# A planned attention-and-MLP kernel on one core: the first step's weights loaded ahead of the chunks, wider zero products, and part of VectorE's early work on ScalarE

## The chip, the core and the metric

The kernel runs on one core of a Trainium2 chip. The core has five engines that run side by side, each through its own list of instructions in order: TensorE (PE in the profile; PEld is its loading of the stationary operand), VectorE (DVE), ScalarE (ACT), GpSimd (POOL) and SyncE (SP), which here only issues transfers. They wait for each other by semaphores. Sixteen DMA engines move data from and to HBM. The metric is the device time of one execution in microseconds; the median of three runs of the kernel before is 622.57 us.

## What is computed

The input is `q`, `k`, `v` of shape (4, 8, 768, 64), a decay `lam` per head, and two weight matrices. A decayed linear attention runs in blocks of 64 positions, and its result goes through a two-layer MLP with a squared ReLU:

```python
for b in range(nb):                      # 12 blocks of 64 positions
    intra = einsum(qb, kb) * Dmask       # Dmask = lam ** rel below the diagonal
    intra = einsum(intra, vb)
    inter = einsum(qb * lam_pow, kv_state)
    out[:, :, sl] = intra + inter
    kv_state = lam_block * kv_state + einsum(kb * rev_pow, vb)
...
h = maximum(x @ w_in, 0)                 # x: 3072 x 512, w_in: 512 x 2048
return (h * h) @ w_out                   # w_out: 2048 x 512
```

## The kernel before

**Work.** The 3072 tokens are 24 chunks of 128 (two attention blocks of one batch each); three chunks make a tile, so there are 8 tiles. The hidden width 2048 is 16 steps of 128. One FFN step of one tile is a first product `mm1` (12 matmuls on 384 columns, lines 429), a ReLU and a square, and a second product `mm2` (lines 435, 436, 438). All matrices of the FFN are kept as a rounded part and a rest (`wih`/`wil`, `woh`/`wol`, `gh`/`gl`), hence three products for each.

**A chunk.** Two transfers of 512 KB bring `ka` and `qv`. `weighted` multiplies the values by the decay table `wdec` that GpSimd makes with two `pow` instructions from the small input `lamx`: for the first six chunks half of the eight head slices on ScalarE (line 326), the rest in one VectorE instruction (line 328). `open` (line 299, matmuls `bank<-qv,ka`) forms scores and state increments; `opened` adds up the states (`hold`, lines 351, 352, 358) and masks the scores (`s`, line 359); `result` (line 299, `bank<-s,qv` and `bank<-qv,hold`) runs in two parts around a tiny ScalarE copy `dot` (line 397); VectorE scales the outcome by `rdec` into `xr` (line 405), ScalarE rounds it into `xs` (line 411) and VectorE takes the rest (line 412).

**Weights.** The matrices arrive as 64-bit floats, 512 KB for each half of a step (32 loads into three buffers `st`). `weights(f, i)` turns a half into float32: ScalarE `Abs` (line 276), four VectorE instructions (lines 277 to 283), a ScalarE cast (line 285) and a VectorE subtraction (line 287). Half 0 of step f is `wih`/`wil`, half 1 is `woh`/`wol`.

**Order.** Nothing is scheduled by a compiler. `Plan` records every operation with an engine, a duration, a key, dependences and buffers, and `Plan.order` plays a list schedule with those numbers; the kernel then issues the instructions in the order that came out. Changed numbers in the plan therefore change the order on the engines, not only the numbers' own lines. Where the plan sees TensorE idle before 140 us of its own time, it writes products of zeros (`filler`, line 237 on 128 rows, line 240 on two halves of 64) into the order. The loads of the first six chunks and the first weights get keys from `load_at` and `ws_at`; a smaller key goes first on SyncE's queue.

Each float32 matmul of lines 237 to 252 and 299 appears twice in the profile's count, together with two loads of the stationary operand: 15 zero products in the order are 30 MATMUL rows and 30 LDWEIGHTS rows.

Of the kernel before, what the change touches and what calls it, by code (L numbers as in the profile page):

```python
# [17 lines left out]
B, H, S, D = 4, 8, 768, 64  # L18
DM, DFF = 512, 2048
P = 128  # L20
# [35 lines left out]
class Plan:  # L56


    LAT = {"PE": 0.22, "ACT": 0.14, "DVE": 0.13, "POOL": 0.12, "SP": 2.3}

    def __init__(self):
        self.ops, self.slots = [], {}
# [11 lines left out]
    def order(self, pe_slow, fill, begin):  # L74
        need, out = {}, {}
        for o in self.ops:
            both = set(map(id, o.deps)) | set(map(id, o.after))
            need[id(o)] = len(both)
            for d in both:
                out.setdefault(d, []).append(o)  # L80
        ready = {e: [o for o in self.ops if o.eng == e and not need[id(o)]] for e in self.LAT}
        free = dict(dict.fromkeys(self.LAT, 0.0), **begin)
        slots = {k: [(0.0, i) for i in range(n)] for k, n in self.slots.items()}
        done, filled, mode = [], 0, None
        while any(ready.values()):
            best = None
            for e, ops in ready.items():
                can = []
                for o in ops:
                    t = max([free[e]] + [d.end + d.lat for d in o.deps])  # L90
                    want = {}
                    for b in o.bufs:
                        if b.slot is None:
                            want[b.kind] = want.get(b.kind, 0) + 1
                    ok = True
                    for k, n in want.items():
                        if len(slots[k]) < n:
                            ok = False
                            break
                        t = max(t, sorted(slots[k])[n - 1][0] + 0.15)  # L100
                    if ok:
                        can.append((t, o))
                if not can:
                    continue
                soon = max(free[e], min(t for t, _ in can)) + 0.05
                t, o = min(((t, o) for t, o in can if t <= soon), key=lambda x: (x[1].key, x[0]))
                if best is None or t < best[0]:
                    best = (t, o)
            assert best is not None, "no operation can get its buffers"
            t, o = best  # L110
            if o.eng == "PE" and t < fill:
                while free["PE"] + (long := FILL * (2.0 if free["PE"] < pe_slow else 1.0)) + FILL_REST < t:
                    bank = min(slots["bank"], default=(t, 0))
                    if bank[0] > free["PE"]:
                        break
                    done.append(Op("PE", long, 0, lambda i=bank[1], m=mode: self.filler(i, m != "A"), [], [], [], 0, None))
                    done[-1].start, done[-1].end = free["PE"], free["PE"] + long
                    free["PE"] += long
                    filled += 1
            dur = o.dur * (2.0 if o.eng == "PE" and t < pe_slow else 1.0)  # L120
            if o.mode:
                dur += SWITCH * (mode not in (None, o.mode))
                mode = o.mode
            o.start, o.end = t, t + dur
            free[o.eng] = o.end
            for b in o.bufs:
                if b.slot is None:
                    slots[b.kind].sort()
                    b.slot = slots[b.kind].pop(0)[1]
                b.left -= 1  # L130
                b.end = max(b.end, o.end + o.lat)
                if not b.left:
                    slots[b.kind].append((b.end, b.slot))
            ready[o.eng].remove(o)
            done.append(o)
            for d in out.get(id(o), ()):
                need[id(d)] -= 1
                if not need[id(d)]:
                    ready[d.eng].append(d)
        assert len(done) - filled == len(self.ops), "operations need each other"  # L140
        return done
# [6 lines left out]
F_LATE = 9  # L148

FIRST, SLOW_STEP, LAG, BEGIN2, CHUNK, STEP = 18.0, 6.5, 16, 9.0, 3.0, 4.8  # L150
PE_SLOW, FILL_END, FILL, FILL_REST, SWITCH = 10.0, 140.0, 0.215, 0.1, 0.18
XOFF = 16
AFTER = NF - 2


# [14 lines left out]
def kernel(ctx: ExitStack, tc: tile.TileContext, ka, qv, lamx, w, out):  # L170
# [61 lines left out]
    def power(hs):  # L232
        nc.gpsimd.tensor_tensor(out=wdec[:, hs], in0=lam[:, hs], in1=ej[:, hs], op=ALU.pow)  # L233

    def filler(i, full):
        if full:
            nc.tensor.matmul(tiles["bank"][i][:, 0:P], zero[:, 0:P], zero[:, P:2 * P], start=True, stop=True)
            return
        for h in range(2):
            nc.tensor.matmul(tiles["bank"][i][half(h), 0:P], zero[half(0), 0:HC], zero[half(0), P:2 * P], start=True, stop=True)  # L240

    plan.filler = filler

    o_start = plan.op("POOL", 5.2, -99, start_tables)
    o_pow = plan.op("POOL", 1.62, -98, lambda: power(slice(0, H)), [o_start])
    o_pow2 = plan.op("POOL", 1.62, -97, lambda: power(slice(H, 2 * H)), [o_pow])
    o_lc = plan.op("POOL", 1.01, -96, lambda: nc.gpsimd.tensor_tensor(out=lc, in0=lam[:, 2 * H:2 * H + NP], in1=ec, op=ALU.pow), [o_pow2])
    wb, rps = Buf("m"), Buf("bank")

# [10 lines left out]
    def weights(f, i, key, load_key):  # L260
# [11 lines left out]
        def add(eng, dur, fn, deps, bufs, lat=None):  # L272
            return plan.op(eng, dur, key, fn, deps, bufs, lat=lat)

        o = plan.op("SP", 1.6, load_key, lambda: nc.sync.dma_start(out=at(st), in_=w[f, i]), [], [st])
        o = add("ACT", 0.56, lambda: nc.scalar.activation(at(m), words(1).bitcast(F32), AF.Abs), [o], [st, m])  # L276
        o = add("DVE", 0.336, lambda: nc.vector.tensor_scalar(
            out=at(m), in0=at(m), scalar1=W_MIN, scalar2=W_MAX, op0=ALU.max, op1=ALU.min), [o], [m])
# [22 lines left out]
    class Chunk:  # L301
# [8 lines left out]
            self.blocks = 2 if self.c < NC_ - 1 else 1  # L310

        def load(self, key):
            self.o_ka = in_turn("load", plan.op("SP", 1.6, key, lambda: nc.sync.dma_start(out=at(self.ka), in_=ka[self.i]), [], [self.ka]))
            self.o_qv = in_turn("load", plan.op("SP", 1.6, key, lambda: nc.sync.dma_start(out=at(self.qv), in_=qv[self.i]), [], [self.qv]))

        def vals(self):
            return at(self.qv)[:, 1].rearrange("p n (h d) -> p n h d", h=2)
# [3 lines left out]

        def weighted(self, key):
            v = lambda: at(self.qv)[:, 1].rearrange("p n (h d) -> p (n h) d", h=2)
            split = H // 2 if self.i < N_ALONE else 0

            self.o_vd = [plan.op("ACT", act(D) + 0.11, key, lambda i=i: nc.scalar.mul(v()[:, i], v()[:, i], wdec[:, i:i + 1]), [self.o_qv, o_pow], [self.qv])
                         for i in range(split)]
            self.o_vd.append(plan.op("DVE", tt((H - split) * D), key, lambda: nc.vector.tensor_tensor(  # L328
                out=v()[:, split:], in0=v()[:, split:], in1=wdec[:, split:H].unsqueeze(2).broadcast_to([P, H - split, D]), op=ALU.mult), [self.o_qv, o_pow], [self.qv]))
# [12 lines left out]
        def opened(self, o, key):  # L342

            s0, s1 = state.get(self.b), Buf("hold")
            self.states, self.o_states = [s0 and s0[0], s1], [s0[1]] if s0 else []
            u = lambda t: at(self.sc[t])[:, NP * HC:].rearrange("p (n d) -> p n d", n=NP)

            def add(t, old, new, deps):

                if old is None:  # L350
                    return plan.op("DVE", tt(256), key, lambda: nc.vector.tensor_copy(at(new), u(t)), [o], [self.sc[t], new])
                return plan.op("DVE", tt(256), key, lambda: nc.vector.tensor_tensor(out=at(new), in0=u(t), in1=at(old), op=ALU.add), [o] + deps, [self.sc[t], new, old])  # L352

            self.o_states.append(add(0, self.states[0], s1, self.o_states))
            if self.blocks == 2:
                new = Buf("hold")
                o1 = add(1, s1, new, self.o_states[-1:])
                state[self.b] = (new, plan.op("DVE", tt(256), key, lambda: nc.vector.tensor_tensor(out=at(new), in0=at(new), in1=lc.unsqueeze(2).broadcast_to([P, NP, D]), op=ALU.mult), [o1, o_lc], [new]))
            self.o_s1 = [in_turn("mask", plan.op("DVE", tt(256), key, lambda h=h: nc.vector.tensor_tensor(
                out=at(self.s1[h]), in0=at(self.sc[h])[:, 0:NP * HC].rearrange("p (n i) -> p n i", n=NP), in1=mask.unsqueeze(1).broadcast_to([P, NP, HC]), op=ALU.mult),  # L360
                [o], [self.sc[h], self.s1[h]])) for h in range(2)]

        def result(self, g, ys):

# [104 lines left out]
                plan.op("SP", 1.0, key, lambda b=b, c=c, row=row: nc.sync.dma_start(  # L469
                    out=out[b * S + c * C:b * S + (c + 1) * C, :], in_=row()), [o], [ob])  # L470

    load_at = [0, 1, 2, 4, 6, 7]
    ws_at = [3, 5] + [8 + f for f in range(NF)]
    per = [SLOW_STEP, SLOW_STEP] + [STEP] * (len(TILES) - 2)
    begin = [FIRST, FIRST + LAG * SLOW_STEP]
    for ti in range(2, len(TILES)):
# [1 line left out]
    ws = []  # L478
    for f in range(NF):
        t = FIRST + f * SLOW_STEP  # L480
        ws.append((weights(f, 0, t - 7, -30 + ws_at[f]), weights(f, 1, t - 2, -30 + ws_at[f] + (2.5 if f == 1 else 0.5))))

    xs_, ready = [Buf("x") for _ in TILES], [[] for _ in TILES]
    chunks = []
# [72 lines left out]
```

## Time and profile before

| | before |
|---|---|
| median of 3 runs (lowest, highest) | 622.57 us (621.34, 624.99) |
| time of the profiled execution | 620.3 us |
| span, first to last instruction, of that execution | 618.5 us |
| mean granted TensorE clock | 0.994 |
| TensorE busy | 607.8 us, 98% of the span |
| VectorE busy | 300.1 us, 49% |
| ScalarE busy | 210.6 us, 34% |
| read from HBM, written | 41.96 MB, 6.29 MB |

In the profile's chain that ended last, time is followed back from the last instruction: at each step to whatever released it. "Issue" in it is time in which an engine waited for nothing that the profile shows. The table of windows gives busy microseconds and, in brackets, the number of instructions of each engine in each stretch, then the granted TensorE clock, the share of DMA time and the rate.

### The profile page before, as it was taken

What the parts mean: (1) busy time and instruction counts of PE and PEld (TensorE: products, weight loads), DVE (VectorE), ACT (ScalarE), POOL (GpSimd) and SP (SyncE); (2) the same over time, 40 slices, a digit from 0 to 9 for tenths busy, and PEclk for the clock granted to TensorE, in tenths of its full rate; (3) what the DMA queues carried; (4) which work ended last, traced back from release to release, by engine and by line L of the source; (5) the groups of instructions that cost most, each with busy time, mean ns of one, the idle gap of its engine ahead of it and who ended that gap; (6) DMA issues with size and microseconds to landing.
All of it is one profiled execution on the core that took longest, in us unless ns stands there. A gap on an engine that the chain in (4) does not pass through costs nothing.

```text
span 618.5 us, 13218 instructions
## 1 busy us (share of the span) xinstructions
PE 607.8 (98%) x5846; PEld 548.1 (89%) x5846; DVE 300.1 (49%) x616; ACT 210.6 (34%) x434; POOL 5.1 (1%) x10
## 2 busy tenths in 40 slices
PE   6899999999999999999999999999999999999997
PEld 6889898988898898998899998989898999899996
DVE  4699999975323444343343442434443433232223
ACT  3347786753342322222223232222223222232221
POOL 3000000000000000000000000000000000000000
PEclk9799999999999999999999999999999999999999
DMA  8465555516110122020121120112210000010001
GB/s 340 174 241 171 171 170 176 195 50 214 62 42 22 65 70 69 35 86 13 57 70 51 70 69 1 69 52 70 69 61 28 34 0 2 1 51 2 1 0 52
DMA packets 15177, 49.10 MB, mean 79 GB/s; under 512 B 1808, under 2 KB 1808, under 8 KB 15120
## 3 DMA queue, kind: packets, MB, share of 16 engines
q1 hardware_dynamic: 14976, 48.24, 22.3%
q8 instruction: 46, 0.75, 0.5%
q14 instruction: 11, 0.09, 0.1%
q10 hardware_dynamic: 144, 0.01, 0.0%
HBM read 41.96 MB, written 6.29 MB: 78 GB/s over the span
## 4 chain that ended last, share of the span: by engine, by line
PE 95%; DMA 2%; issue 1%; DVE 0%; ACT 0%; POOL 0%; POOLq 0%; SPq 0%; ACTq 0%
PE bank L429 43%; PE bank L435 14%; PE bank L438 14%; PE bank L436 14%; PE bank L299 8%; PE bank L240 2%; DMA qv<-qv 1%; DMA st<-w 1%; DMA g<-lamx 1%; POOL wdec L233 0%; POOLq L553 0%; PE bank L252 0%; DVE xr L468 0%; DVE qv L328 0%; ACT m L276 0%
## 5 line engine op out<-in xcount | busy, mean ns | idle before, releaser
L429 PE MATMUL bank<-xs,wih 128*128 128x384 f32 x1024 | 200.5, 338 | 0.0
L429 PEld LDWEIGHTS bank<-xs,wih 128*128 128x128 f32 x1024 | 180.6, 188 | 6.5 <-issue 0.2
L443 ACT ACTIVATE g<-bank 128x384 f32<-128x384 f32 x128 | 62.8, 491 | 271.9 <-PE bank L429 271.7
L449 DVE TENSOR_TENSOR g<-g 128x384 f32<-128x384 f32 x96 | 53.5, 558 | 207.2 <-ACT gh L448 161.5
L435 PE MATMUL bank<-woh,gh 128*128 128x512 f32 x384 | 152.0, 396 | 0.0
L436 PE MATMUL bank<-wol,gh 128*128 128x512 f32 x384 | 150.8, 393 | 0.0
L429 PE MATMUL bank<-xs,wil 128*128 128x384 f32 x512 | 110.1, 337 | 0.0
L438 PE MATMUL bank<-woh,gl 128*128 128x512 f32 x384 | 109.3, 393 | 0.1
L429 PEld LDWEIGHTS bank<-xs,wil 128*128 128x128 f32 x512 | 91.1, 188 | 0.0
L438 PEld LDWEIGHTS bank<-woh,gl 128*128 128x128 f32 x384 | 71.7, 188 | 16.9 <-DVE gl L450 1.0
L435 PEld LDWEIGHTS bank<-woh,gh 128*128 128x128 f32 x384 | 72.1, 188 | 14.1
L436 PEld LDWEIGHTS bank<-wol,gh 128*128 128x128 f32 x384 | 72.1, 188 | 13.4
L450 DVE TENSOR_TENSOR gl<-g,gh 128x384 fp32r<-128x384 f32 x128 | 71.3, 557 | 22.2 <-ACT gh L446 13.7
L448 ACT ACTIVATE gh<-g 128x384 fp32r<-128x384 f32 x96 | 50.3, 524 | 3.0
L411 ACT CAST xs<-xr 128x512 fp32r<-128x512 f32 x24 | 14.9, 621 | 46.6 <-DVE xr L405 46.6
L352 DVE TENSOR_TENSOR hold<-bank,hold 128x256 f32<-128x256 f32 x40 | 16.7, 418 | 25.9 <-PE bank L299 25.8
L328 DVE TENSOR_TENSOR qv<-qv,wdec 128x512 f32<-128x512 f32 (+1 forms) x24 | 15.0, 624 | 28.1 <-DMA qv<-qv 23.9
L299 PE MATMUL bank<-qv,ka 64*64 64x64 f32 x1472 | 28.3, 224 | 0.0
L299 PEld LDWEIGHTS bank<-qv,ka 64*64 64x64 f32 x1472 | 26.1, 140 | 0.6 <-issue 0.4
L276 ACT ACTIVATE m<-st 128x512 f32<-128x512 f32 x32 | 21.6, 675 | 8.0 <-DMA st<-w 7.8
L299 PEld LDWEIGHTS bank<-s,qv 64*64 64x64 f32 x768 | 17.8, 138 | 7.3 <-issue 5.3
L299 PE MATMUL bank<-s,qv 64*64 64x64 f32 x768 | 23.5, 232 | 0.3 <-ACT dot L397 0.3
(46 smaller groups left out, 310.7 us busy)
## 6 DMA issues: line engine op xcount, KB each, us to landing
st<-w SPq DMA_DIRECT2D x32, 512.0 KB, 3.5
ka<-ka SPq DMA_DIRECT2D x24, 512.0 KB, 3.7
qv<-qv SPq DMA_DIRECT2D x24, 512.0 KB, 5.2
out<-ob SPq DMA_DIRECT2D x23, 256.0 KB, 2.3
out<-xr SPq DMA_DIRECT2D x1, 256.0 KB, 2.0
g<-lamx ACTq DMA_DIRECT2D x1, 12.0 KB, 4.1
```

What stands on the lines that cost most here:

```text
L276: o = add("ACT", 0.56, lambda: nc.scalar.activation(at(m), words(1).bitcast(F32), AF.Abs), [o], [st, m])
L299: nc.tensor.matmul(*args, **kw, skip_group_check=True)
L328: self.o_vd.append(plan.op("DVE", tt((H - split) * D), key, lambda: nc.vector.tensor_tensor(out=v()[:, split:], in0=v()[:, split:], in1=wd ...
L352: return plan.op("DVE", tt(256), key, lambda: nc.vector.tensor_tensor(out=at(new), in0=u(t), in1=at(old), op=ALU.add), [o] + deps, [self.s ...
L429: nc.tensor.matmul(at(h)[:, 0:N], wt[:, cc, :], xt[:, cc, :], start=k == 0, stop=k == 3 * NCC - 1)
L435: nc.tensor.matmul(at(os_[j]), at(gh)[:, sl], woh[f], start=f == 0, stop=False)
L436: nc.tensor.matmul(at(os_[j]), at(gh)[:, sl], wol[f], start=False, stop=False)
L438: nc.tensor.matmul(at(os_[j]), at(gl)[:, sl], woh[f], start=False, stop=f == NF - 1)
L443: orr = plan.op("ACT", 0.49, key, lambda: nc.scalar.activation(at(g), at(h)[:, 0:N], AF.Relu), [o1], [h, g, run])
L448: ogh = plan.op("ACT", 0.525, key, lambda: nc.scalar.activation(at(gh), at(g), AF.Square), [orr], [g, gh])
L449: og = plan.op("DVE", 0.555, key, lambda: nc.vector.tensor_tensor(out=at(g), in0=at(g), in1=at(g), op=ALU.mult), [orr, ogh], [g])
L450: ogl = plan.op("DVE", 0.555, key, lambda: nc.vector.tensor_tensor(out=at(gl), in0=at(g), in1=at(gh), op=ALU.subtract), [og, ogh], [g, gh, ...
```

## The change

Four things are edited, and the plan's numbers with them:

1. `load_at` and `ws_at` put both halves of step 0's weights ahead of every chunk, and half 0 of step 1 between chunks 1 and 2; the conversions follow in the order, since the plan lets them start when they land.
2. A zero product may have 128, 256, 384 or 512 columns; the plan writes one wide product where it wrote up to four narrow ones.
3. `split` goes from 4 to 6 (`VS`): for the first six chunks six of eight head slices are weighted on ScalarE. The first state of a batch is copied from PSUM by ScalarE instead of VectorE (four copies). Score masks are taken for half 1 first.
4. The plan's own numbers: load 1.6 to 1.28, latency after a load 2.3 to 2.0, the GpSimd table 5.2 to 4.95, `PE_SLOW` 10 to 6.5. They set no instruction, only the order.

```diff
-    LAT = {"PE": 0.22, "ACT": 0.14, "DVE": 0.13, "POOL": 0.12, "SP": 2.3}
+    LAT = {"PE": 0.22, "ACT": 0.14, "DVE": 0.13, "POOL": 0.12, "SP": 2.0}
...
-                while free["PE"] + (long := FILL * (2.0 if free["PE"] < pe_slow else 1.0)) + FILL_REST < t:
+                while True:
+                    unit = FILL * (2.0 if free["PE"] < pe_slow else 1.0)
+                    n = min(4, int((t - FILL_REST - free["PE"]) / unit))
                     bank = min(slots["bank"], default=(t, 0))
-                    if bank[0] > free["PE"]:
+                    if n < 1 or bank[0] > free["PE"]:
                         break
...
-PE_SLOW, FILL_END, FILL, FILL_REST, SWITCH = 10.0, 140.0, 0.215, 0.1, 0.18
+PE_SLOW, FILL_END, FILL, FILL_REST, SWITCH = 6.5, 140.0, 0.215, 0.1, 0.18
+VS = 6
...
-            nc.tensor.matmul(tiles["bank"][i][half(h), 0:P], zero[half(0), 0:HC], zero[half(0), P:2 * P], start=True, stop=True)
+            nc.tensor.matmul(tiles["bank"][i][half(h), 0:n * P], zero[half(0), 0:HC], zero[half(0), 0:n * P], start=True, stop=True)
...
-            split = H // 2 if self.i < N_ALONE else 0
+            split = VS if self.i < N_ALONE else 0
...
                 if old is None:
-                    return plan.op("DVE", tt(256), key, lambda: nc.vector.tensor_copy(at(new), u(t)), [o], [self.sc[t], new])
+                    return plan.op("ACT", act(256), key, lambda: nc.scalar.copy(at(new), u(t)), [o], [self.sc[t], new])
...
-                [o], [self.sc[h], self.s1[h]])) for h in range(2)]
+                [o], [self.sc[h], self.s1[h]], [] if h or s0 else [o1])) for h in (1, 0)]
...
-    load_at = [0, 1, 2, 4, 6, 7]
-    ws_at = [3, 5] + [8 + f for f in range(NF)]
+    load_at = [1, 2, 4, 5, 7, 8]
+    ws_at = [0, 3] + [9 + f for f in range(NF)]
...
-        ws.append((weights(f, 0, t - 7, -30 + ws_at[f]), weights(f, 1, t - 2, -30 + ws_at[f] + (2.5 if f == 1 else 0.5))))
+        ws.append((weights(f, 0, t - 7, -30 + ws_at[f]), weights(f, 1, t - 2, -30 + ws_at[f] + (3.5 if f == 1 else 0.5))))
```

Line numbers after the change are higher by three or four (299 becomes 302, 429 becomes 433).

**SyncE's queue at the start.** The names are the buffers: `ka_2` and `qv_2` are chunk 2's two transfers, `st` the weights. Before, from the fifth load on (the four of chunks 0 and 1 stand ahead):

```order
L313 DMA ka_2_150<-ka 128x1024
L314 DMA qv_2_156<-qv 128x1024
L275 DMA st_133<-w 128x512
L275 DMA st_134<-w 128x512
L313 DMA ka_3_151<-ka 128x1024
L314 DMA qv_3_157<-qv 128x1024
L275 DMA st_135<-w 128x512
L313 DMA ka_4_152<-ka 128x1024
L314 DMA qv_4_158<-qv 128x1024
L313 DMA ka_5_153<-ka 128x1024
L314 DMA qv_5_159<-qv 128x1024
L275 DMA st_133<-w 128x512
```

Now, from the first load on:

```order
L278 DMA st_133<-w 128x512
L278 DMA st_134<-w 128x512
L316 DMA ka_0_148<-ka 128x1024
L317 DMA qv_0_154<-qv 128x1024
L316 DMA ka_1_149<-ka 128x1024
L317 DMA qv_1_155<-qv 128x1024
L278 DMA st_135<-w 128x512
L316 DMA ka_2_150<-ka 128x1024
L317 DMA qv_2_156<-qv 128x1024
L316 DMA ka_3_151<-ka 128x1024
L317 DMA qv_3_157<-qv 128x1024
L278 DMA st_133<-w 128x512
```

Chunks 0 and 1 moved back by two loads, chunk 2 by three, chunks 3 to 5 by one; the fourth weight load (`st_133` for the second time) was the sixteenth and is the twelfth. Chunks 4 and 5, two more weight loads and both transfers of chunks 6 and 7 follow it.

**TensorE around the second part of chunk 4's result.** `bank<-s_1,qv_4` and `s_0,qv_4` end chunk 4, `s_2,qv_5` and `s_3,qv_5` begin the result of chunk 5, `ob` is the buffer of zeros. Before:

```order
L299 MATMUL bank_66<-s_1_121,qv_4_158 64x64 x2
L299 MATMUL bank_65<-s_0_120,qv_4_158 64x64 x2
L240 MATMUL bank_61<-ob_114 64x128 x26
L299 MATMUL bank_61<-s_2_122,qv_5_159 64x64 x2
L299 MATMUL bank_62<-s_3_123,qv_5_159 64x64 x2
```

Now:

```order
L302 MATMUL bank_66<-s_0_120,qv_4_158 64x64 x2
L302 MATMUL bank_67<-s_1_121,qv_4_158 64x64 x2
L433 MATMUL bank_62<-xs,wih_73 128x384 x8
L433 MATMUL bank_62<-xs,wil_74 128x384 x4
L302 MATMUL bank_61<-s_3_123,qv_5_159 64x64 x2
L302 MATMUL bank_63<-s_2_122,qv_5_159 64x64 x2
```

The last 26 zero products are gone, and the first product of step 1 of tile 0 stands there. In the whole order the zero products go from 103 (15 of 128 rows and 88 of 64) to 23 (7 and 16), and ahead of the first FFN step from 77 to 23; after that step there are none now.

**ScalarE ahead of the first FFN step.** `m` is a weight half under conversion, `g` the hidden values of the first step. Before:

```order
L285 CAST wih_69<-m_137 128x512
L411 CAST xs<-xr_3_163 128x4x128
L326 ACTIVATE qv_5_159<-qv_5_159,wdec 128x64 x4
L276 ACTIVATE m_137<-st_133 128x512
L443 ACTIVATE g_111<-bank_64 128x384
L445 ACTIVATE g_111<-g_111 128x384
```

Now, at its beginning, behind the table load:

```order
L279 ACTIVATE m_136<-st_133 128x512
L279 ACTIVATE m_137<-st_134 128x512
L288 CAST wih_69<-m_136 128x512
L329 ACTIVATE qv_0_154<-qv_0_154,wdec 128x64 x6
L288 CAST woh_71<-m_137 128x512
L354 COPY hold_125<-bank_61 128x256
```

Step 0's conversions moved to the head of the list, ahead of the weighting of chunk 0; `Abs` of the fourth weight half (`m_137<-st_133`), which stood just ahead of the first step's ReLU, now stands fifteen rows ahead of it. The two halves of step 2 (`m_138<-st_134`, `m_136<-st_135`) now stand two and three rows ahead of that ReLU.

More of the change, by code (lines that the diff above doesn't have):

```diff
@@ L111, in order @@
             if o.eng == "PE" and t < fill:
-                while free["PE"] + (long := FILL * (2.0 if free["PE"] < pe_slow else 1.0)) + FILL_REST < t:
+                while True:
+                    unit = FILL * (2.0 if free["PE"] < pe_slow else 1.0)
+                    n = min(4, int((t - FILL_REST - free["PE"]) / unit))
                     bank = min(slots["bank"], default=(t, 0))
-                    if bank[0] > free["PE"]:
+                    if n < 1 or bank[0] > free["PE"]:
                         break
-                    done.append(Op("PE", long, 0, lambda i=bank[1], m=mode: self.filler(i, m != "A"), [], [], [], 0, None))
-                    done[-1].start, done[-1].end = free["PE"], free["PE"] + long
-                    free["PE"] += long
+                    done.append(Op("PE", n * unit, 0, lambda i=bank[1], m=mode, n=n: self.filler(i, m != "A", n), [], [], [], 0, None))
+                    done[-1].start, done[-1].end = free["PE"], free["PE"] + n * unit
+                    free["PE"] += n * unit
                     filled += 1
@@ L233, in power, with filler @@
         nc.gpsimd.tensor_tensor(out=wdec[:, hs], in0=lam[:, hs], in1=ej[:, hs], op=ALU.pow)
-    def filler(i, full):
+    def filler(i, full, n):
         if full:
-            nc.tensor.matmul(tiles["bank"][i][:, 0:P], zero[:, 0:P], zero[:, P:2 * P], start=True, stop=True)
+            nc.tensor.matmul(tiles["bank"][i][:, 0:n * P], zero[:, 0:P], zero[:, 0:n * P], start=True, stop=True)
             return
         for h in range(2):
-            nc.tensor.matmul(tiles["bank"][i][half(h), 0:P], zero[half(0), 0:HC], zero[half(0), P:2 * P], start=True, stop=True)
+            nc.tensor.matmul(tiles["bank"][i][half(h), 0:n * P], zero[half(0), 0:HC], zero[half(0), 0:n * P], start=True, stop=True)
     plan.filler = filler
-    o_start = plan.op("POOL", 5.2, -99, start_tables)
-    o_pow = plan.op("POOL", 1.62, -98, lambda: power(slice(0, H)), [o_start])
-    o_pow2 = plan.op("POOL", 1.62, -97, lambda: power(slice(H, 2 * H)), [o_pow])
+    o_start = plan.op("POOL", 4.95, -99, start_tables)
+    o_pow = plan.op("POOL", 1.6, -98, lambda: power(slice(0, H)), [o_start])
+    o_pow2 = plan.op("POOL", 1.6, -97, lambda: power(slice(H, 2 * H)), [o_pow])
     o_lc = plan.op("POOL", 1.01, -96, lambda: nc.gpsimd.tensor_tensor(out=lc, in0=lam[:, 2 * H:2 * H + NP], in1=ec, op=ALU.pow), [o_pow2])
@@ L273, in add @@
             return plan.op(eng, dur, key, fn, deps, bufs, lat=lat)
-        o = plan.op("SP", 1.6, load_key, lambda: nc.sync.dma_start(out=at(st), in_=w[f, i]), [], [st])
+        o = plan.op("SP", 1.28, load_key, lambda: nc.sync.dma_start(out=at(st), in_=w[f, i]), [], [st])
         o = add("ACT", 0.56, lambda: nc.scalar.activation(at(m), words(1).bitcast(F32), AF.Abs), [o], [st, m])
@@ L312, in load @@
         def load(self, key):
-            self.o_ka = in_turn("load", plan.op("SP", 1.6, key, lambda: nc.sync.dma_start(out=at(self.ka), in_=ka[self.i]), [], [self.ka]))
-            self.o_qv = in_turn("load", plan.op("SP", 1.6, key, lambda: nc.sync.dma_start(out=at(self.qv), in_=qv[self.i]), [], [self.qv]))
+            self.o_ka = in_turn("load", plan.op("SP", 1.28, key, lambda: nc.sync.dma_start(out=at(self.ka), in_=ka[self.i]), [], [self.ka]))
+            self.o_qv = in_turn("load", plan.op("SP", 1.28, key, lambda: nc.sync.dma_start(out=at(self.qv), in_=qv[self.i]), [], [self.qv]))
         def vals(self):
```

## The prediction

> **What bounds the kernel now.** I read the page first, then the chain of waits of the first 60 us, then a table of windows cut where that chain has holes. The page says that TensorE is nearly always busy:
>
> ```profile
> span 618.5 us, 13218 instructions
> PE 607.8 (98%) x5846; PEld 548.1 (89%) x5846; DVE 300.1 (49%) x616; ACT 210.6 (34%) x434; POOL 5.1 (1%) x10
> q8 instruction: 46, 0.75, 0.5%
> ```
>
> The chain (start, length, what) shows where it is not, or is busy with zeros (line 240):
>
> ```profile
> 12.27 2.78 issue
> ...
> 19.49 1.59 issue
> ...
> 30.01 5.22 DMA st<-w
> ...
> 37.50 2.83 PE bank L240 x52
> 40.33 0.89 PE bank L299 x48
> ...
> 44.09 6.24 PE bank L429 x36
> ```
>
> From 44.09 the chain is TensorE's matmuls in close order, so what follows is fixed work. The end moves by as much as the start of that run moves, and everything the change is worth must come from the first 44 us. These, cut at the holes (start:end, length, then busy time and count of PE, PEld, DVE, ACT, POOL, granted clock, DMA share, GB/s):
>
> ```profile
> 0.00:12.27 12.27, 10.37 (x222) 9.75 (x223) 5.55 (x19) 4.74 (x15) 5.08 (x10) 1.00 0.85 324
> 12.27:15.04 2.77, 0.00 (x1) 0.00 (x0) 2.05 (x7) 0.67 (x1) 0.00 (x0) 1.00 1.02 404
> 15.04:19.49 4.45, 4.43 (x128) 3.73 (x127) 2.12 (x6) 2.57 (x7) 0.00 (x0) 0.62 1.03 408
> 19.49:21.06 1.57, 0.00 (x0) 0.00 (x0) 1.57 (x5) 0.03 (x1) 0.00 (x0) 1.00 1.02 407
> 21.06:31.79 10.73, 10.72 (x324) 10.33 (x324) 7.20 (x20) 3.38 (x11) 0.00 (x0) 0.84 0.15 50
> 31.79:43.91 12.12, 11.46 (x267) 10.15 (x266) 11.43 (x27) 6.01 (x15) 0.00 (x0) 1.00 0.76 270
> ```
>
> Between the two holes TensorE executed 128 + 127 = 255 instructions, and 222 + 223 = 445 ahead of the first. The page's queue q8 moved 46 packets of instructions in 0.75 MB, 16 KB each; TensorE's 2 x 5846 instructions divided by 46 are 254. So a packet holds one such stretch, and in both holes TensorE waited for its next 255 instructions while the DMA share was 1.02: the packet stood among the loads. One block took 15.04 to 21.06, 6.0 us, under full load. After a hole the clock drops (0.62, then 0.84, a loss of 0.38 x 4.45 + 0.16 x 10.73 = 3.4 us).
>
> The Trainium skill, "Runtime: NRT & Kernel Launch", section "Instruction fetch mechanics", says that the sequencer fetches blocks of 16 KiB, 256 instructions, by a DMA queue of its own, and that this is hidden. The size agrees with the 255 of this trace; that it is hidden does not, by 2.77 and 1.57 us.
>
> **The change part by part.** The rows for the first loads and the steps around them (start, length; waits in brackets):
>
> ```profile
> 5.04 3.24 POOL L233 TENSOR_TENSOR wdec<-g 128x8 f32<-128x8 f32 x2 [2.84 <-DMA g<-lamx]
> 6.70 0.43 DVE L328 TENSOR_TENSOR qv<-qv,wdec 128x256 f32<-128x256 f32 x1 [4.08 <-POOL wdec L233]
> 7.01 1.38 PE L299 MATMUL bank<-qv,ka 64*64 64x64 f32 x64
> 8.56 1.06 ACT L326 ACTIVATE qv<-qv,wdec 128x64 f32<-128x64 f32 x4 [0.79 <-DMA qv<-qv]
> 11.13 0.59 ACT L326 ACTIVATE qv<-qv,wdec 128x64 f32<-128x64 f32 x2 [1.51 <-DMA qv<-qv]
> 12.41 0.67 ACT L276 ACTIVATE m<-st 128x512 f32<-128x512 f32 x1 [0.16 <-DMA st<-w]
> 31.80 1.65 PE L429 MATMUL bank<-xs,wih 128*128 128x384 f32 x8
> 35.31 0.69 ACT L276 ACTIVATE m<-st 128x512 f32<-128x512 f32 x1 [2.09 <-DMA st<-w]
> ```
>
> *Loads.* The fourth, sixth and seventh load of the queue release ScalarE at 8.56, 11.13 and 12.41: 1.28 us each. Chunk 0's `qv` was second and becomes fourth (8.56), chunk 1's becomes sixth (11.13), chunk 2's ninth (11.13 + 3 x 1.28 = 15.0, was 11.13). Step 0's weights become first and second (about 4.7 and 6.0). Before, SyncE stopped after 15 loads until a weight buffer came free at 30.01; now 22 loads run without that stop, to about 8.56 + 18 x 1.28 = 31.6, so the load on the DMA engines lasts some 9 us longer.
>
> *Chunk 0.* Six slices on ScalarE cost 1.06 x 6/4, about 1.6 us, where four cost 1.06; they stand behind the first weight cast, so they start near 8.6, and `open` follows at about 10.5 instead of 7.01: +3.5 us.
>
> *Prices of the moved pieces:*
>
> ```profile
> L351 DVE COPY hold<-bank 128x256 f32<-128x256 f32 x4 | 1.7, 420 | 1.0 <-PE bank L299 1.0
> L281 DVE SCALAR_TENSOR_TENSOR m<-st,m 128x512 uint32<-128x512 uint32 x3 | 2.1, 685 | 0.0
> L277 DVE TENSOR_SCALAR m<-m 128x512 f32<-128x512 f32 x4 | 1.7, 418 | 0.0
> L287 DVE TENSOR_TENSOR wil<-m,wih 128x512 fp32r<-128x512 f32 x2 | 1.4, 688 | 0.1
> L411 ACT CAST xs<-xr 128x512 fp32r<-128x512 f32 x5 | 3.1, 620 | 2.9 <-DVE xr L405 2.9
> L397 ACT COPY dot<-bank 128x1 f32<-128x1 f32 x6 | 0.9, 153 | 12.5 <-PE bank L299 12.5
> L240 PE MATMUL bank<-ob 64*64 64x128 f32 x176 | 12.8, 290 | 4.4 <-issue 4.4
> ```
>
> A state copy on ScalarE lies between 0.15 (one column) and 0.62 us (512); I take 0.35, for 256 columns; VectorE masks meanwhile, so per chunk it is worth -0.3 to +0.2 and I take 0. VectorE's weighting of two slices lies between nothing and the 0.43 of four, and is cheaper by 0 to 0.4. Step 0's conversions on VectorE (two halves of 2 x 0.42 + 3 x 0.69 = 2.9 us) move into the first 12.27 us, where VectorE was busy 5.55; without that cover they would push chunks 0 and 1 back by as much as 2 us. `Abs` of the fourth weight half, which held ScalarE 2.09 us ahead of the first ReLU, is then loaded long before.
>
> *Zero products.* A 128-column one took 2.83/52 = 0.054 us per record; one of 512 columns takes between that (if the count sets it) and 0.218 (if the columns do); I take 0.218, as 128 columns already cost 0.054. Those behind chunk 2's result then hold TensorE about 1.5 us; the wait for a block, below, covers that, and if the wait is gone they cost it. What counts is their number: each zero product is four instructions. Ahead of the first FFN step there were 77 and are 23: 216 instructions fewer. By the windows that step was instruction 445 + 255 + 648 = 1348; it becomes about 1132. It stood behind the block ends at 445, 700, 956 and 1212, and now behind the first three.
>
> *Sum.* (a) I take the block after 445 to be asked for while `open` of chunk 0 runs, since that work stands 255 instructions ahead of its end; then it comes 3.5 us later: 15.04 + 3.5 = 18.5. (b) The loads no longer pause, so I give each next block the 6.0 us of the loaded case: 24.5 and 30.5. (c) From 956 to 1132 the order has the end of chunk 3's first result part, chunk 4's `open` and a second result part, no zeros: about 1.4 us by the 1.38 of the `open` row, hence the first FFN step at 31.9, against 31.80: +0.1. (d) From 31.79 to 43.91 TensorE was idle 12.12 - 11.46 = 0.66 and spent 2.83 on zeros; both go, since step 1's first product now stands where the zeros stood: -3.5. (e) Block 1212 comes at about 30.5 + 4 (the loads end at 31.6) and is wanted near 34.4: 0, or up to +2 under full load. Sum +0.1 - 3.5 + 0 = **-3.4 us**: 616.9 instead of 620.3 for the profiled execution, and 619.2 on the median of 622.57, which lies 2.3 us above it. A difference under 0.5% (3.1 us) can hardly be told from none in this kernel.
>
> **The rivals.**
>
> *Faster: no block is waited for.* If fewer instructions or other gaps between loads let the blocks through, the two holes (2.78 + 1.59) and the clock loss (3.4) vanish and the later load of chunk 2 (15.0 - 11.1) is paid: 31.8 - 7.8 + 3.9 = 27.9 for the first step, -3.9 - 3.5 = -7.4, 615.2. This is what the page's "hidden" would give. For it speaks the smaller number of instructions; against it that the DMA share is 1.0 for longer. Chance 0.20.
>
> *Slower: the blocks take longer.* With T per block for all three, the first step comes at 18.5 + 2T + 1.4, which is 2T - 11.9 against 31.8, and block 1212 at 18.5 + 3T for a want 2.5 us behind that step, T - 3.9 more: with (d) the sum is 3T - 19.3. At T = 6.0 that is -1.3, at 6.4 zero, from 7.5 on slower by 0.5%: +3.2, 625.8. The first block before bears on T: its predecessor was entered at or after 7.01 and it came at 15.04, at most 8.0 us. Against it: the 6.0. Chance 0.12.
>
> *No change: VectorE takes over.* The weights of steps 1 to 15 are converted while TensorE runs two tiles:
>
> ```profile
> 80.00:100.00 20.00, 20.00 (x103) 18.21 (x102) 19.65 (x39) 14.86 (x30) 0.00 (x0) 1.00 0.56 177
> ```
>
> VectorE is at 98% there. An earlier TensorE could outrun it and give the 3.4 us back: 622.6. Against it: VectorE sheds four copies (1.7) and has 5.8 us of step 0 behind it when the run begins. Chance 0.16.
>
> *GpSimd and VectorE in each other's way.* VectorE's first seven conversion instructions (4 x 0.42 + 3 x 0.69 = 3.8 us) now fall on the two `pow` instructions (5.04 to 8.28). If they were held until 8.28, chunk 0's weighting would follow at 12.1, `open` at 12.3 instead of 10.5: +1.8, sum -1.6, 621.0. The only such pair in the trace, L328 at 6.70, took 0.43 inside a `pow`, no more than elsewhere. Chance 0.06. The Trainium skill, "SBUF — State Buffer", sections on the shared port pair, says that a VectorE instruction with two SBUF inputs and a GpSimd one that reads SBUF block each other wholly; by L328's row the trace does not show it.
>
> **How the numbers follow.** The forecast (-3.4, by itself from -5.5 with an earlier block to -1.4 with (e) at +2) has 0.46, of which 0.28 lies beyond 3.1 us. Faster by over 0.5%: 0.28 + 0.20 = 0.48. Slower: 0.10 of the 0.12. The rest, 0.18 + 0.16 + 0.06 + 0.02 = 0.42, is the same. The range takes in the fast rival and stops short of the slow one's end: 614.8 to 623.2.
>
> **What would show it.** Right: the first FFN product at 31 to 33 us; a hole on TensorE behind some 445 + 255 instructions, in `open` of chunk 3; DMA share 1.0 to about 31 us; no zeros after the first step; `Abs` of the fourth half without a wait; the close run of matmuls reached with about 3.5 us less spent. Wrong: no hole, or holes at other counts (then my account of blocks fails); new VectorE waits ahead of TensorE's second products between 45 and 110 us; L280 to L286 stretched while `pow` runs.

## The result, and the profile after

The changed kernel took **618.91 us** (median of nine runs, 617.25 to 619.88); the kernel before took 621.86 beside it (nine runs, 619.43 to 624.99). The ratio is 0.9948, 95% interval [0.9925, 0.9971]. The profiled execution took 618.99 us, against 620.3 before.

The page's lines that answer to those of before:

```profile
span 617.3 us, 12907 instructions
PE 606.9 (98%) x5686; PEld 538.4 (87%) x5686; DVE 298.0 (48%) x612; ACT 215.1 (35%) x450; POOL 5.7 (1%) x10
q8 instruction: 44, 0.72, 0.5%
```

TensorE has 160 matmul records fewer. The chain of waits of the changed kernel (start, length, what):

```profile
17.88 1.78 issue
...
23.57 2.37 issue
...
28.48 1.92 PE bank L243 x5
...
30.60 0.85 PE bank L243 x2
...
34.56 2.28 PE bank L433 x12
...
38.87 2.29 PE bank L433 x12
...
46.94 6.24 PE bank L433 x36
```

Both holes are still there, later. The `DMA st<-w` piece at 30.01 and the zeros at 37.50 of before are gone. But the wide zeros (L243) now stand on the chain, and the first FFN product (L433) comes later than before. The table of windows, cut at the holes, with the columns as before:

```profile
0.00:17.88 17.88, 15.62 (x222) 8.33 (x223) 12.86 (x33) 10.56 (x30) 5.74 (x10) 1.00 0.88 350
17.88:19.66 1.78, 0.01 (x1) 0.00 (x1) 1.43 (x5) 0.52 (x2) 0.00 (x0) 1.00 1.02 407
19.66:23.57 3.91, 3.72 (x127) 3.30 (x127) 1.29 (x4) 2.28 (x8) 0.00 (x0) 0.61 1.04 414
23.57:25.94 2.37, 0.00 (x0) 0.00 (x0) 1.50 (x4) 0.81 (x2) 0.00 (x0) 0.92 1.01 398
25.94:34.49 8.55, 8.50 (x218) 5.96 (x217) 4.26 (x12) 5.05 (x18) 0.00 (x0) 0.60 0.62 244
34.49:46.60 12.11, 12.11 (x241) 10.41 (x235) 12.10 (x30) 6.15 (x14) 0.00 (x0) 1.00 0.13 46
80.00:100.00 20.00, 20.00 (x104) 18.26 (x103) 19.58 (x39) 14.61 (x28) 0.00 (x0) 1.00 0.55 186
```

222 + 223 = 445 instructions stand ahead of the first hole, 127 + 127 between the two. Ahead of the first FFN product the clock is 0.60, while TensorE is busy for 8.50 of 8.55 us. Behind it TensorE is busy throughout. VectorE is busy 19.58 of 20 us between 80 and 100, but TensorE has no gap there.

The clock of 1.00 in the first row of such a table needs a note. The traces record the clock only from some 4.4 to 7.7 us on (6.87 in the changed kernel), and ahead of that the zeros run at half rate: in the kernel before, one 128-column record starts every 213 ns up to 5.5 us, and every 112 ns from 5.7 us on.

### The profile page after: what moved, and what is told of

Read it like the earlier page. It is cut to its first block, busy times and chain, and to the rows that moved or that the text cites. A ratio compares the mean times of both kernels' runs of the same rounds, so it can differ in the third digit from the quotient of the medians.

```text
span 617.3 us, 12907 instructions
## 1 busy us (share of the span) xinstructions
PE 606.9 (98%) x5686; PEld 538.4 (87%) x5686; DVE 298.0 (48%) x612; ACT 215.1 (35%) x450; POOL 5.7 (1%) x10
## 3 DMA queue, kind: packets, MB, share of 16 engines
q1 hardware_dynamic: 14976, 48.24, 21.4%
## 4 chain that ended last, share of the span: by engine, by line
PE 96%; DMA 2%; DVE 1%; issue 1%; ACT 0%; ACTq 0%
PE bank L433 44%; PE bank L439 15%; PE bank L442 14%; PE bank L440 14%; PE bank L302 8%; DMA ka<-ka 1%; DMA g<-lamx 1%; PE bank L243 1%; DVE m L284 0%; DVE xr L472 0%; DVE s L363 0%; DVE xr L409 0%; DVE rdec L260 0%; DVE m L282 0%; DVE hold L361 0%
## 5 line engine op out<-in xcount | busy, mean ns | idle before, releaser
L433 PE MATMUL bank<-xs,wih 128*128 128x384 f32 x1024 | 200.7, 338 | 0.0
L433 PEld LDWEIGHTS bank<-xs,wih 128*128 128x128 f32 x1024 | 180.6, 188 | 6.0
L433 PE MATMUL bank<-xs,wil 128*128 128x384 f32 x512 | 110.0, 337 | 0.0
L433 PEld LDWEIGHTS bank<-xs,wil 128*128 128x128 f32 x512 | 91.0, 188 | 0.0
L302 PE MATMUL bank<-s,qv 64*64 64x64 f32 x768 | 23.1, 232 | 2.7 <-issue 1.8
L331 DVE TENSOR_TENSOR qv<-qv,wdec 128x512 f32<-128x512 f32 (+1 forms) x24 | 14.1, 590 | 24.0 <-DMA qv<-qv 23.9
```

Of the source, the lines that this page charges most:

```text
L302: nc.tensor.matmul(*args, **kw, skip_group_check=True)
L433: nc.tensor.matmul(at(h)[:, 0:N], wt[:, cc, :], xt[:, cc, :], start=k == 0, stop=k == 3 * NCC - 1)
```

## The experiments

Theory A is the prediction's: TensorE's instructions ahead of the first FFN product, fetched in blocks under the loads, set when that product starts, and the new load order removes the waits behind it. Theory B: the load order is the gain, the zeros do nothing. Theory C: what moves is the TensorE clock. Each time below has its ratio to the kernel before in the same series, with the 95% interval. "First" is the start of the first FFN product; "behind" is the span less that start; "lost" is TensorE's idle time up to its last product, and its zeros; "half" is the time at half clock, as far as the trace records the clock. These four are of the one profiled execution, whose own time lies within 2.1 us of the median; all in us. "Clock" below is the mean granted TensorE clock of one run.

| kernel | median | ratio | first | behind | lost | half |
|---|---|---|---|---|---|---|
| before | 621.86 | 1 | 31.80 | 586.7 | 23.7 | 6.8 |
| changed | 618.91 | 0.9948 [0.9925, 0.9971] | 34.49 | 582.8 | 21.2 | 10.2 |
| 1 wide zeros alone | 617.56 | 0.9927 [0.9900, 0.9955] | 28.39 | 586.9 | 21.9 | 0 |
| 2 changed, narrow zeros | 621.25 | 0.9984 [0.9967, 1.0001] | 35.47 | 583.6 | 23.1 | 10.2 |
| 3 changed, old loads | 618.93 | 0.9948 [0.9929, 0.9966] | 31.92 | 586.2 | 22.6 | 13.7 |
| 4 changed, old split | 619.96 | 0.9965 [0.9945, 0.9985] | 35.84 | 581.8 | 22.4 | 10.2 |
| 5 load order alone | 621.06 | 0.9991 [0.9973, 1.001] | 34.28 | 587.1 | 24.4 | 13.7 |
| 6 ScalarE part alone | 622.22 | 1.0 [0.9977, 1.0023] | 33.93 | 585.4 | 25.0 | 13.7 |
| 7 no late zeros | 623.16 | 1.0016 [1.0, 1.0031] | 32.50 | 588.4 | 25.1 | 10.2 |
| 8 changed, whole-array zeros | 618.42 | 0.9938 [0.9919, 0.9957] | 32.81 | 582.6 | 20.6 | 6.8 |
| 9 = 8 with old loads | 619.67 | 0.9955 [0.9936, 0.9973] | 28.47 | 590.8 | 24.5 | 6.8 |
| 10 = 8, chunks 3 to 5 later | 619.49 | 0.9946 [0.9924, 0.9967] | 31.96 | 584.7 | 21.4 | 6.8 |
| 11 = 1 with whole-array zeros | 618.10 | 0.9927 [0.9902, 0.9951] | 28.99 | 587.6 | 21.4 | 3.4 |
| 12 = 8, order between | 620.72 | 0.9974 [0.9958, 0.9989] | 29.01 | 590.3 | 22.4 | 3.4 |

### 1. Wide zero products alone, on the kernel before

```diff
-  tiles["bank"][i][half(h), 0:P], ... zero[half(0), P:2 * P]
+  tiles["bank"][i][half(h), 0:n * P], ... zero[half(0), 0:n * P]   # n up to 4, as in the change
```

> The kernel before, with zero products of up to 512 columns as the only edit: 36 zero products instead of 103, everything else in the same order. Blocks theory (the start is set by when TensorE's blocks of 255 instructions arrive among the loads): fewer instructions stand ahead of the first FFN step, so it comes behind one block less; one hole of about 2 us instead of two, first step at 29 to 30.5 us instead of 31.8, time 1.5 to 2.5 us less. Order theory (the whole gain comes from what the new order has behind the first step): 0, within 0.7 us.

Its windows, cut at its holes:

```profile
13.63:15.36 1.73, 0.00 (x1) 0.00 (x0) 1.05 (x4) 0.00 (x0) 0.00 (x0) 1.00 1.02 405
15.36:20.44 5.08, 4.95 (x128) 2.94 (x127) 3.90 (x11) 2.62 (x7) 0.00 (x0) 1.00 1.03 407
20.44:21.39 0.95, 0.01 (x1) 0.01 (x1) 0.95 (x4) 0.00 (x0) 0.00 (x0) 1.00 1.02 410
21.39:28.39 7.00, 7.00 (x227) 4.44 (x227) 5.95 (x16) 3.41 (x11) 0.00 (x0) 1.00 0.17 51
```

The fourth weight half is still waited for in its chain of waits, as before:

```profile
32.99 5.16 DMA st<-w
```

With 1153 instructions ahead of the first product instead of 1349, that product starts 3.4 us earlier, and the stretch behind it is unchanged (586.9). Two holes stay, where one was expected, and the gain is 4.4 us, where 1.5 to 2.5 was. The blocks come no earlier: the holes end at 15.36 and 21.39, against 15.04 and 21.06 before, and they are shorter (1.73 and 0.95, against 2.78 and 1.59) because TensorE reaches them later. What shrinks is the stretch from the second hole to the first product, from 10.73 to 7.00 us. It has 454 instructions instead of 648, and its clock is 1.00 instead of 0.84, which by 0.16 x 10.73 is 1.7 of these 3.7 us.

The runs, too, show the clock beside the count. At a clock of 0.994, two runs of this kernel took 619.11 and 619.65 us, and four of the kernel before 620.44 to 621.34: about 1.3 us less. The other 3 of the 4.4 us go with the clock, which is 0.994 to 1.000 in the six runs of this kernel and 0.986 to 0.994 in the 27 of the kernel before. So this one edit gives no less than the whole change, and theory B falls; theories A and C both have a part in it.

### 2 to 4. The change with one part undone

```diff
2: -  n = min(4, int((t - FILL_REST - free["PE"]) / unit))
2: +  n = min(1, int((t - FILL_REST - free["PE"]) / unit))
3: -  load_at = [1, 2, 4, 5, 7, 8]; ws_at = [0, 3] + ...
3: +  load_at = [0, 1, 2, 4, 6, 7]; ws_at = [3, 5] + ...
4: -  split = VS;      nc.scalar.copy(at(new), u(t));        for h in (1, 0)
4: +  split = H // 2;  nc.vector.tensor_copy(at(new), u(t)); for h in range(2)
```

> The changed kernel with zero products of 128 columns only: 67 instead of 23, the same columns in all. Blocks theory: the first FFN step stands one block further back, first step 2 to 4 us later than 34.5, 2 to 4 us slower than the changed kernel. Order theory: no difference. Clock theory (wide zero products on half of the rows leave the clock at half rate): one half-rate window of 3.4 us fewer, 1 to 1.7 us faster.

> The changed kernel with the loads in the old order (chunks 0 to 2 ahead of the first weights). Blocks theory: chunk 0 opens 2.5 to 3.5 us earlier and with it the first block, so the first step comes 2 to 4 us earlier, but zeros or waits return behind it; in all within 1.5 us of the changed kernel. Theory that the early weights carry the gain: 2 to 4 us slower, near the kernel before.

> The changed kernel with four slices on ScalarE, state copies on VectorE and the old order of the masks. Blocks theory: the counts ahead of the first step hardly change, so 0 to 1 us slower. Theory that VectorE's relief carries the gain: VectorE is later by four copies (1.7 us) and the wider weightings (up to 0.9 us) in the first 35 us, 1.5 to 3 us slower.

Narrow zeros take most of the gain away, 2.3 us: 1309 instructions stand ahead of the first product, and a third hole comes where the count says, at 955 (chain of waits):

```profile
20.00 1.75 issue
...
24.31 3.52 issue
```

The first product is only 1.0 us later than in the changed kernel, where 2 to 4 was expected; the stretch behind it is 0.8 longer. Here the clock is not the cause: at a clock of 0.992, four runs of kernel 2 took 620.12 to 620.80 us and three of the changed kernel 618.28 to 618.99.

Undoing the load order brings the first product forward by 2.6 us (34.49 to 31.92), lengthens what lies behind it by 3.4 (582.8 to 586.2) and leaves the median where it was. Undoing the ScalarE part costs 1.05 us in the medians, with intervals that overlap; 1269 instructions then stand ahead of the first product instead of 1133, so the counts did change.

### 5 and 6. The load order alone, the ScalarE part alone

```diff
5: -  load_at = [0, 1, 2, 4, 6, 7]; ws_at = [3, 5] + [8 + f ...]; 2.5 if f == 1
5: +  load_at = [1, 2, 4, 5, 7, 8]; ws_at = [0, 3] + [9 + f ...]; 3.5 if f == 1
6: -  split = H // 2; nc.vector.tensor_copy(at(new), u(t)); for h in range(2)
6: +  split = 6;      nc.scalar.copy(at(new), u(t));        for h in (1, 0)
```

> The kernel before with the new load order alone (first step's weights first). Theory A (the order shortens what lies behind the first FFN product by 3 to 4 us and makes that product 3 to 4 us later): first FFN product at 35 to 36 us, from there to the end 583.0 to 583.8 us, 621 to 622. Theory B (the order is where the change's gain comes from): first product at 32 to 33, 618 to 619. Theory C (with 64-row zeros of 128 columns the instructions ahead of the first product are 1349 or more, so a third hole falls ahead of it, as with narrow zeros in the changed kernel): holes after 445, 701 and 955, 622 to 624.

> The kernel before with the ScalarE part alone (six heads' weighting and the first states on ScalarE, second mask first). Taken out of the changed kernel it cost 1.05 us (619.96 against 618.91). Theory A (it takes VectorE's chain off the first step whatever the load order): first FFN product 1 to 2 us earlier than 31.8, 620 to 621. Theory B (TensorE's order and the fetch holes set the first product in the old order, with 1349 instructions ahead of it): same, 621.9 +- 0.7. Theory C (with less waiting, the zeros fewer and the holes elsewhere, the clock has another number of half-rate windows): 619 to 623 with the clock to show it.

Neither gives anything that can be measured. For 5, theory A's time came out, but not what it rested on: the first product came at 34.28, before the 35 to 36 expected, and the stretch behind it did not shorten. A hole now falls into it, in 5's chain of waits (after 1720 instructions, which is 190 + 6 x 255), and 3.4 us at half clock follow:

```profile
34.35 2.29 PE bank L429 x12
...
38.90 2.29 PE bank L429 x12
...
42.51 1.92 issue
```

For 6, theory A failed: the first product came 2.1 us later, not earlier. The time fits theories B and C; the first product at 33.93 speaks against B, and the clock is there as C had it: the runs go from 622.6 to 626.2 at clocks of 0.986 to 620.1 to 622.2 at 0.991 and 0.992.

### 7. No zero products behind the first FFN step, on the kernel before

```diff
-  FILL_END = 140.0
+  FILL_END = 28.0
```

> The kernel before with zero products only in the planned first 28 us, so that the 52 products behind the first FFN product (2.83 us) are left out. Theory A (they fill time in which TensorE waits for VectorE and the fourth weight half, and cost nothing themselves): idle time of about 3.3 us instead of 0.66 behind the first product, time 621.9 +- 0.6. Theory B (the term of 2.83 us in the prediction is a cost of the products themselves): 619.1. Theory C (without them the clock window falls to half rate behind the first product): one or two more half-rate windows, 622.5 to 624.

Idle time of 3.51 us took the place of 0.72 idle and 2.83 of zeros, as theory A had it, and a window at half clock followed (41.31 to 44.72), as theory C had it; the time, 623.16, is C's. So those zeros cost nothing where they stood; what cost was the wait, which they filled.

### 8 and 9. Every zero product over the whole array

```diff
-  if full:
+  if True:      # 128 rows at once, not two products of 64 rows
```

> The changed kernel, with every zero product over the whole array (128 rows, one product instead of two of 64 rows each). Theory A (the half-rate windows cost the first step, and zero products of 64 rows do not bring the clock back): the windows of 27.35 to 34.17 us stay at full rate, at most one half-rate window is left, mean clock 0.997 or more against 0.992, first FFN product at 32 to 33 us instead of 34.49. Over the nine runs of the changed kernel the time falls by 2.5 us for each 0.010 of mean clock (619.9 at 0.986, 617.25 at 0.996), which gives 616.4 at 1.000: expected 616.5 to 617.2. Theory B (the holes at every 255th instruction are the loss and also set the half-rate windows, whatever the zeros are): the two holes stay after instructions 445 and about 699, half-rate windows follow them as before, 618.9 +- 0.5. Rival C (a product over the whole array between 64-row ones costs a switch): each of the some ten places pays about 0.2 us, first product later, 619.5 to 621.

> The changed kernel with the load order of before and every zero product over the whole array. Theory A (64-row zeros kept the clock at half rate for 13.65 us of the old-order run): none or one half-rate window is left, first FFN product at 28 to 30 us instead of 31.92; the ten runs of that kernel fall by 2.0 us for each 0.010 of clock to 617.7 at 1.000, so 617.5 to 618. Theory B (the clock follows idle time alone): 618.9 as with the 64-row zeros. If it comes below 616.5, the old order is the better one once the clock holds.

The half-rate windows lie on a grid of 3.41 us. The changed kernel's windows on that grid, then those of kernel 8:

```profile
17.11:20.52 3.41, 1.34 (x38) 0.75 (x36) 2.20 (x6) 1.21 (x6) 0.00 (x0) 1.00 1.03 410
20.52:23.93 3.41, 3.04 (x103) 2.86 (x104) 1.65 (x5) 2.43 (x8) 0.00 (x0) 0.50 1.02 406
23.93:27.35 3.42, 1.41 (x79) 1.41 (x80) 1.64 (x5) 1.01 (x3) 0.00 (x0) 1.00 1.03 405
27.35:30.76 3.41, 3.41 (x38) 1.54 (x32) 2.48 (x8) 2.76 (x11) 0.00 (x0) 0.50 0.99 388
30.76:34.17 3.41, 3.36 (x100) 2.76 (x100) 1.15 (x4) 1.41 (x6) 0.00 (x0) 0.50 0.16 56
```

```profile
23.35:26.76 3.41, 1.48 (x62) 1.25 (x62) 1.98 (x6) 1.27 (x4) 0.00 (x0) 1.00 1.01 401
26.76:30.17 3.41, 3.41 (x43) 2.13 (x33) 1.65 (x6) 2.09 (x8) 0.00 (x0) 0.50 1.04 411
30.17:33.59 3.42, 3.42 (x119) 2.70 (x118) 2.75 (x8) 2.37 (x9) 0.00 (x0) 1.00 0.23 86
```

A window with a hole in it (busy 1.34, 1.41, 1.48 of 3.41) is followed by one at 0.50. In the changed kernel the window at 27.35, busy throughout, for 2.67 us of it with 64-row zeros, does not bring the clock back; in kernel 8 the one at 26.76, with 2.31 us of whole-array zeros, does, and the first product comes 1.7 us earlier: about 0.5 by the blocks, and from instruction 955 on 1.2 us for 146 instructions instead of 2.35 for 178. By these two profiles both theories had a part: a hole stands ahead of the first half-rate window, 64-row zeros ahead of the second. Theory A's clock and time did not come: the six runs have 0.992 to 0.994, not 0.997, and the profiled one, at 617.09, is the fastest of them. In the medians (618.42 against 618.91, intervals overlapping) the edit is not resolved. Rival C, a price for each switch, does not show. Kernel 9 did not reach its 617.5: its first product is the earliest but one, and 3.0 us idle and 3.8 of zeros behind it, with a hole after 1210 instructions, take it back.

### 10 to 12. Three tries for less

```diff
10: -  BEGIN2 = 9.0
10: +  BEGIN2 = 18.0
12: -  load_at = [1, 2, 4, 5, 7, 8]; ws_at = [0, 3] + ...; 3.5 if f == 1
12: +  load_at = [0, 2, 3, 5, 7, 8]; ws_at = [1, 4] + ...; 2.5 if f == 1
```

> The changed kernel with every zero product over the whole array, and chunks 3 to 5 put off in the plan (BEGIN2 18 instead of 9), so that chunk 4's open and the last part of chunk 3 (80 products, 160 instructions) stand behind the first FFN product instead of ahead of it. Theory A (instructions ahead of that product are what the fetch holes limit): about 940 instructions ahead instead of 1101; holes stay after 445 and 700 and no third comes; first product at 31 to 32 us instead of 32.8; the work put off fills TensorE's wait for the second step's weights, so what lies behind lengthens by the 80 products (1.4 us) at most: 617 to 618.4. Theory B (the first product waits for VectorE's chain of chunk 2 and the weights, not for TensorE): first product at 32.8 still, 1.4 us more behind it, 619.5 to 620. As the plan's own times have it, the end is 0.5 later: 618.9.

> The kernel before with wide zero products only, and these over the whole array. With 64-row wide zeros it took 617.56. Theory A (clock: whole-array zeros hold it): clock 0.997 or more in most runs, 616.3 to 617.3. Theory B (the gain of wide zeros is the count of instructions ahead of the first FFN product alone): some 30 instructions fewer than 1153, holes at the same counts, 617.0 to 618.0. Rival C (as in the changed kernel with the old order, whole-array zeros shift the work so that a hole comes in chunk 3 or behind the first product, with a half-rate window after it): 618.5 to 620.

> A try for a version below both: the changed kernel with whole-array zeros and a load order between the two (chunk 0, first step's two halves, chunks 1 and 2, third half, chunk 3, fourth half, chunks 4 and 5). Theory A (the two orders trade the first product, early with chunks first, against what lies behind it, short with the weights first; an order between takes part of both): first FFN product at 30 to 31 us, from there to the end 584 to 585 us, 615.5 to 617.5. Theory B (the time follows where the holes after instructions 445, 700 and 955 fall and how many half-rate windows follow them, which no order of loads sets by itself): holes at these counts, two or three half-rate windows, clock 0.992 to 0.994, 618 to 619.5.

In 10, 160 instructions fewer made the first product 0.85 us earlier, and what they did came behind it (+2.1): nothing won, though the first product lies where theory A had it. 11 is level with 1: its clock is 0.997 or more in all six runs, as theory A had it, but its time is not lower, so a fuller clock alone brought no gain here. 12 started early with one half-rate window and still came out slower than both theories had it: a hole after 1209 instructions, the second step's product only at 39.55, and 4.8 us of idle time and zeros behind the first product. A short half-rate time is therefore not enough; why its runs end some 2 us above kernel 8's, I did not settle. No kernel beat the wide zeros alone (617.56), whose interval overlaps that of the change.

## Why the prediction was right, step by step

**The number.** 619.2 was forecast, 618.91 measured. But the sum, -3.4 us, was made for the profiled execution, and that went from 620.3 to 618.99, -1.3. The other 2 us came from the offset: I carried over the 2.3 us by which the profiled execution of before lay under its median of three, while the changed kernel's lies 0.1 above its own. Runs of one kernel differ with the clock: the nine of the changed kernel go from 617.25 at a mean clock of 0.996 to 619.88 at 0.986, and 27 of the kernel before, in the series of kernels 1 to 4, from 620.4 to 621.3 at 0.994, where its profile was taken, to 625.6 and 625.9 at 0.986. The forecast landed with two errors that cancel, and that it came within 0.3 us is luck. At one clock the change is worth about 3 us: at 0.992, three of its runs took 618.28 to 618.99, and three of those 27 took 620.57 to 622.53. So the size of the sum is near, but not what it is made of.

**(a) First block at 18.5.** It came at 19.66. The step that failed is the rule "asked for while `open` of chunk 0 runs". These two traces fit another: the block comes some 6 us after TensorE enters the one before it. Instruction 191 (445 - 255 = 190 stand ahead of it) starts at 8.90 before, and the hole ends 6.15 later; in the changed kernel it starts at 13.44, and the hole ends 6.22 later. Over all fourteen profiles this first distance is 4.6 to 6.2 us, so the 6 is no constant, and what sets it stays open. `open` itself came earlier than I said, at 9.50 instead of 10.5.

**(b) 6.0 us per block.** The second came at 25.94, 6.28 later; instruction 955 starts at 32.14, another 6.20, after a wait of 0.05. In the eleven profiles with a wait at both 445 and 700 the distance is 6.02 to 6.45 us. The rival of slower blocks has T = 6.28 in its formula, 3T - 19.3 = -0.5; but no hole came at 1212, so (e), 0, holds.

**(c) First product at 31.9.** It came at 34.49, 2.6 us later: 1.16 from (a), 0.48 from (b), and 0.95 from the stretch behind instruction 955, 2.35 us where I had 1.4, with the clock at half until 34.17. The sum had no term for half clock, though I had read a loss of 3.4 us by it off the profile of before. In kernel 8, at full clock, that stretch took 1.2 us for 146 instructions, which at the same rate would be 1.5 for the 178 of the changed kernel (an estimate).

**(d) -3.5 behind the first step.** Idle time and zeros there went from 0.72 + 2.83 to nothing, and the stretch behind went from 586.7 to 582.8. Size and place are right. Kernel 3 shows that it hangs on the load order, since with the old one 0.5 of idle time and 2.8 of zeros are back; kernel 5 shows that the load order does not do it alone, kernel 7 that the zeros as such were no cost.

**What I gave no weight.** I counted the 216 instructions fewer and used the count only to place the product among the blocks. By kernels 1 and 2 the narrow zeros are the lever: wide ones alone give 4.4 us, of which about 1.3 at the same clock, and narrow ones cost the changed kernel 2 us at the same clock. The split between count and clock rests on a few runs each. The rival "no block is waited for" had fewer instructions as a cause at a chance of 0.20. In kernel 1 its clock loss did vanish, but both holes stayed; in the whole change the later chunks and half clock took the gain ahead of the first product back.

**The other rivals.** VectorE did not take over: TensorE has no gap from 34.49 on, and none between 80 and 100. GpSimd and VectorE held each other up little: of the first seven conversions six ran inside the two `pow` of the changed kernel and the seventh began there, all at their usual length; the two `pow` grew from 3.24 to 3.50 us, and the next GpSimd instruction, for `lc`, from 1.01 to 1.40 (start, length):

```profile
5.26 3.50 POOL L236 TENSOR_TENSOR wdec<-g 128x8 f32<-128x8 f32 x2 [3.07 <-DMA g<-lamx]
5.65 0.43 DVE L280 TENSOR_SCALAR m<-m 128x512 f32<-128x512 f32 x1 [3.03 <-ACT m L279]
6.57 0.69 DVE L284 SCALAR_TENSOR_TENSOR m<-st,m 128x512 uint32<-128x512 uint32 x1
8.73 1.40 POOL L250 TENSOR_TENSOR lc<-g 128x4 f32<-128x4 f32 x1
```

## What to carry to other kernels

At a kernel's start, while the loads fill the DMA engines, TensorE's instructions are themselves a load: where TensorE waited for two blocks of 255 in a row, they came 6.0 to 6.5 us apart here, so instructions that do nothing, zeros for the clock above all, should be few and wide. Judge a reordering by the start of the closely packed run plus what is idle behind it, since moving a load here only shifted time from one to the other. And before adding a profile's offset to a forecast, see whether that execution had a typical clock.

## What the hardware showed that I had not expected

- Half clock follows windows that are far from idle. Over the first 65 us of the fourteen profiles, 20 of the 22 full-rate windows with TensorE busy for 0.18 to 0.57 of 3.41 us are followed by one at half clock; of eight at 0.58 to 0.78, one. The Trainium skill, "TensorE: Matmul & The Clock Gate", section "What's actually happening", says that the window is 3413 ns, runs freely, and that half clock comes after an idle window. The length agrees with the 3.41 of the traces; the condition does not, by the 1.41 us of work in the window at 23.93.
- How far a product reaches over the array matters for the way back. In the five kernels with whole-array zeros all eight stretches at half clock are one window long; in the nine others seven of thirteen are two to four long. The changed kernel and kernel 8 differ in this edit alone (which also takes 32 instructions away), as do 3 and 9, and 1 and 11: in these pairs the lowest clock of any run goes from 0.986 to 0.992, from 0.989 to 0.993 and from 0.994 to 0.997. That the rows are the reason is argued from this, not shown apart from the count.
- The same hole costs more or less by where it lies on the grid. In kernel 1 the hole at 13.63 lies across a border, leaves the window at 14.1 busy for 0.59, and no half clock follows.
